# Projecting three tiles of the first head block in float32 from host-transposed copies, and splitting w1 by column blocks

## The chip, the cores and the metric

The kernel runs on one core of a Trainium2 chip. The metric is the time of one execution on the device, in microseconds (us). Engines are named as the profile names them: PE (TensorE matmuls), PEld (its weight loads), DVE (VectorE), ACT (ScalarE), POOL (GpSimd) and SP (SyncE, which here issues the DMAs).

## The reference

The input x is 2048 tokens of 512 features, all float32. What is computed is

```
xn = layernorm(x)
s  = attention(xn) @ wo      # 32 heads of 16; token p looks at p, p-2, ..., p-14 (W = 8, dilation 2)
y  = layernorm(xn)
g  = silu(gelu(y @ w1 + b1) @ w2 + b2)      # 512 -> 1376 -> 512
out = x + s * g
```

with q, k, v = xn @ wqkv, logits scaled by 1/4, positions below 0 masked, and softmax over the 8 positions.

## The kernel before

**Tiles and units.** Tokens are split by parity (the dilation is 2) into two halves of 8 tiles, each of 128 tokens. The 32 heads are split into four head blocks of eight. A unit is one half with one head block; there are eight, u = 0 to 7. `qkv(c, hb, u)` projects a unit's 8 tiles into the buffer U[u % 2] (128 partitions, q, k and v side by side), `attention(c, hb, u)` works on it: products and reductions on DVE, exp on ACT, part of the sums on POOL. The MLP is 44 steps, four chunks of 512 tokens by 11 blocks of F: `mlp1` (12 matmuls, gelu on ACT, high and low part), `mlp2` (12 matmuls into four PSUM tiles). `wo_first` and `wo_last` apply wo.

**Split precision.** A float32 operand is scaled by a power of two and split into a float16 high part and a float16 low part; a product is three float16 matmuls (high by high, low by high, high by low). So a tile's projection is 12 matmuls of 384 columns (line 632). The scale is found on the device: a square with accumulation on ACT (lines 465, 383), a sum over partitions by a small float32 matmul against a tile of fours (lines 391, 396), four short DVE operations (402 to 420). High parts come from ACT (483, 436) or DVE (434), low parts from DVE (485, 437).

**The first layer norm.** `ln0` takes the tiles of the first half in groups (GROUPS): statistics on DVE (525, 526), powers on POOL (512, 519), the normalised tile on DVE (564) or ACT (531, 534). The tile is then transposed on PE by four float32 transposes (571) into PSUM and split into the float16 parts of yT (ACT 581, DVE 582). Two tiles, FP = (2, 3), go first: their transposes are copied to SBUF in float32 (577) and multiplied directly with the unscaled float32 weights (line 639, four matmuls a tile), so that unit 0 can begin before its weights are scaled and split. Evictions to U are on ACT (648). U[1] also holds head block 1's raw weights until they are split. The second half's layer norm (`ln1`) transposes by DMA.

**Order.** Every operation is added to a plan (`Plan.add`) with an engine, an assumed duration, a priority and what it reads and writes. `Plan.issue` then plays the plan through: at each step it takes, over all engines, the operation that can start first, among those nearly as early the one of lowest priority number, and so fixes each engine's order of instructions, which buffer of a ring each gets, and the order of SP's DMAs. On the chip each engine works through its order and waits where an operand is late. PE gets fillers (`WAKE`, line 1042: matmuls of fours into a PSUM tile that nobody reads) where the plan has nothing else for it.

**w1.** The host lays w1 out as 128 partitions by four K tiles of 1376 columns. It is loaded in four pieces, squared in four, and split in four (W1C): since a piece is a range of K, the first MLP step needs parts of all of them.

Of the kernel before, what the change touches and what calls it, by code (L numbers as in the profile page):

```python
# [18 lines left out]
P = 128  # L19
# [5 lines left out]
NI = 8  # L25
# [8 lines left out]
W1C = [0, 2048, 4096, 5120, KT * F]  # L34
LAG = 2
# [3 lines left out]
GROUPS = [(2,), (3,), (0, 1), (4, 5), (6, 7)]  # L39
LOADS = [(2, 1), "q0", "q2", (3, 1), (0, 2), (4, 2), (6, 2)]  # L40

FP = (2, 3)

ACT_Y = (0, 1, 4, 5)

W1DVE = (0, 1, 2, 3)
# [6 lines left out]

DVE_LO = range(0, 44)

# [27 lines left out]
class Plan:  # L83
# [76 lines left out]
    def earliest(self, o):  # L160
        t = max(self.free[o.eng], o.ready)
        if o.port:
            t = max(t, self.portfree)
        if o.eng == "sp" and o.nbytes and len(self.landed) >= QUEUE:
            t = max(t, self.landed[-QUEUE])
        return t

    def place(self, o, t):

        if o.eng == "sp":  # L170
            if not o.nbytes:
                return t
            self.free["sp"] = t + o.issue
            self.dma = max(self.dma, t + o.issue + 0.3)
            self.dma += o.nbytes / (o.rate if self.dma > SLOW else 265e3)
            end = self.dma + o.tail
            self.landed.append(end)
            return end
# [78 lines left out]
MARGIN = {"pe": 0.2, "dve": 0.15, "act": 0.05}  # L257
# [3 lines left out]
QUEUE = 8  # L261

PW2, PS2 = 0.9, 0.74
PWQ1, PW1 = 0.7, 0.75
# [4 lines left out]
WAKE = 4  # L269
WAKE0 = 22  # L270
# [6 lines left out]
PFP = 0.62  # L277
# [13 lines left out]
def tile_mixer(ctx, tc, a_x, a_wqkv, a_wo, b_w1, b_b1, b_w2, out):  # L291
# [21 lines left out]
    def act(n, fn, r, w, aps=1, **k):  # L313
        pl.add("act", 0.07 + n * ACT1 + 0.093 * aps, fn, r, w, **k)
# [13 lines left out]
    fours = sb.tile([P, P], F32, name="fours")  # L328
    nc.vector.memset(fours, 4.0)
    halves = sb.tile([P, 16], F32, name="halves")  # L330
# [8 lines left out]
    w1 = sb.tile([P, 2, KT, F], F16, name="w1")  # L339
# [18 lines left out]
    R_w = Ring(sb, [P, 16], F32, 8, "lw")  # L358
# [27 lines left out]
    def total(dst, dkey, cols, n, ckeys, late=False):  # L386

        b = (R_ps if late else R_z[0]).new()
        if n == 2:
            for k in range(2):  # L390
                pl.add("pe", 0.15, lambda k=k: nc.tensor.matmul(
                    b.t[:, 0:1], fours, cols()[:, k:k + 1], start=(k == 0), stop=(k == 1)),
                    [ckeys[k]], [b], prio=min(pl.prio, PTOT))
            n = 1
        else:
            pl.add("pe", 0.3, lambda: nc.tensor.matmul(b.t[:, 0:n], fours, cols()[:, 0:n], start=True,
                                                       stop=True), ckeys, [b], prio=min(pl.prio, PTOT))
        src, skey = (lambda: b.t[:, 0:1]), b
        if n > 1:
# [3 lines left out]
                                               op0=ALU.max, op1=ALU.min), [skey], [dkey])  # L403

    def half_exp(ss, skey):
# [4 lines left out]
                                                      op=ALU.logical_shift_right), [skey], [b])  # L410
        return h, b

    def up(dst, dkey, h):

        dve(1, lambda: nc.vector.tensor_scalar(dst.bitcast(I32), h[0](), -TWO23, 205.0 * TWO23,
                                               op0=ALU.mult, op1=ALU.add), [h[1]], [dkey])
# [43 lines left out]
    def prep_q(hb):  # L460
# [9 lines left out]
        with pl.fuse():  # L470
            total(lambda: ssq[:, hb:hb + 1], ("ssq", hb), lambda: col.t, 2, [(col, 0), (col, 2)],
                  late=hb > 1)
            h = half_exp(lambda: ssq[:, hb:hb + 1], ("ssq", hb))
            up(qsc[:, hb, 0:1], ("qs", hb), h)
            down(qsc[:, hb, 1:2], ("qi", hb), h, 24.0)
        st = 1 if hb == 0 else 2
# [14 lines left out]
    cpos = [2, 3, 0, 1, 4, 5, 6, 7]  # L491


    def factors(n, mv, mk, cdst, ckeys, bias=True, close=None, pp=None, **k):
# [19 lines left out]
        with pl.fuse():  # L514
            dve(n, lambda: nc.vector.tensor_scalar(a0(), V(), EPS, None, op0=ALU.add), mk, [(A, 0)])
            dve(n, lambda: nc.vector.reciprocal(a1(), a0()), [(A, 0)], [(A, 1)])
            dve(n, lambda: nc.vector.tensor_tensor(a1(), a1(), V(), op=ALU.mult), [(A, 1)] + mk, [(A, 1)])
            dve(n, lambda: nc.vector.tensor_scalar(a1(), a1(), EPS, None, op0=ALU.add), [(A, 1)], [(A, 1)])
# [4 lines left out]
    def stats(mv, a, key, x, xkeys, **k):  # L523
        st = R_bn.new()
        dve(512, lambda: nc.vector.bn_stats(st.t, x()), xkeys, [st], port=False)  # L525
        dve(8, lambda: nc.vector.bn_aggr(mv()[:, a], st.t), [st], [key], port=False, c=0.08, **k)
# [11 lines left out]
    yF = {}  # L538

    def ln0(ii, xs, xkeys):  # L540
        n = len(ii)
        first, way = dict(prio=PLN + pl.prio * 1e-3), dict(prio=PLN + 0.03 + pl.prio * 1e-3)
        mvb = R_w.new()
        mv = lambda: mvb.t.rearrange("p (i s) -> p i s", s=2)
        mk = [(mvb, a) for a in range(n)]

        behind = [("yd", i) for i in (2, 3) if n > 1]
        fz = pl.fuse()
        for a in range(n - 1):
            with pl.fuse():  # L550
                stats(mv, a, mk[a], xs[a], [xkeys[a]] + behind)
        fz.__enter__()
        stats(mv, n - 1, mk[n - 1], xs[n - 1], [xkeys[n - 1]] + behind)
        rb = factors(n, mv, mk, cT[:, 0, cpos[ii[0]]:cpos[ii[0]] + n], [("c", 0, i) for i in ii],
                     ii[0] in ACT_Y, lambda: fz.__exit__(None, None, None), **{"pp": first["prio"]})
        for a, i in enumerate(ii):
            y = R_f.new()
            o = (i % 4) * P
            dst = yT[i // 4]
            if ii[0] in ACT_Y:  # L560
                with prio(PLN + 0.04):
                    y_act(xs[a], rb, a, [xkeys[a]], lambda y=y: y.t, y, ("y_", i))
            else:
                dve(512, lambda a=a, y=y: nc.vector.tensor_scalar(
                    y.t, xs[a](), mv()[:, a, 0:1], rb[0].t[:, a:a + 1], op0=ALU.subtract,
                    op1=ALU.mult), [xkeys[a], (rb[0], 0)] + mk, [y, ("yd", i)], f=0.72, **first)
            b = R_z[1 + i % 3].new()

            def tr(b=b, y=y):
                for k in range(KT):  # L570
                    nc.tensor.transpose(b.t[:, k * P:(k + 1) * P], y.t[:, k * P:(k + 1) * P], ident)
            pe(4, P, tr, [y], [b], fp32=2, **first)
            p3 = lambda b=b: b.t.rearrange("p (k t) -> p k t", k=KT)
            hi, lo = dst[:, 0, :, o:o + P], dst[:, 1, :, o:o + P]
            if i in FP:
                yf = yF[i] = R_L.new()
                act(512, lambda b=b, yf=yf: nc.scalar.copy(yf.t, b.t), [b], [yf], aps=0, **way)
                p3, b, way2 = (lambda yf=yf: yf.t.rearrange("p (k t) -> p k t", k=KT)), yf, dict(prio=PFP)
            else:
                way2 = way  # L580
            act(512, lambda p3=p3, hi=hi: nc.scalar.copy(hi, p3()), [b], [("yh", 0, i)], aps=0, **way2)
            dve(512, lambda p3=p3, hi=hi, lo=lo: nc.vector.tensor_tensor(  # L582
                lo, p3(), hi, op=ALU.subtract), [b, ("yh", 0, i)], [("y", 0, i)], port=i in FP, **way2)

# [24 lines left out]
    IORD, IORD0 = [2, 3, 1, 4, 5, 6, 7, 0], [2, 3, 0, 1, 4, 5, 6, 7]  # L609

    def qkv(c, hb, u):
        ub = u % 2
        U3 = U[ub].rearrange("p (s e) -> p s e", e=P)
        cs = R_cs.new()
        act(NI, lambda: nc.scalar.activation(cs.t, cT[:, c], AF.Identity, scale=qsc[:, hb, 1:2]),
            [("c", c, i) for i in range(NI)] + [("qi", hb)], [cs], prio=PEV) if u else [
            dve(len(g), lambda q=cpos[g[0]], n=len(g), g=g: nc.vector.tensor_scalar(
                cs.t[:, q:q + n], cT[:, c, q:q + n], 1.0 / YS if g[0] in FP else qsc[:, hb, 1:2], None, op0=ALU.mult),
# [617 lines left out]
```

## Time and profile before

| | us |
|---|---|
| median of 3 runs | 420.17 (419.83 to 420.49) |
| the profiled execution | 419.94 |
| its span in the profile | 418.2 |
| PE busy | 408.5 |
| DVE busy | 384.2 |
| ACT busy | 214.8 |
| POOL busy | 111.4 |

The profile is of one execution. A row of the timeline gives the start, the duration from the first to the end of the last of a run of equal instructions, the engine, the line, what is written from what is read, and how many; in brackets the idle time ahead of it and what ended it. A row of the windows gives the stretch and its length, then the busy time and count of PE, PEld, DVE, ACT and POOL, the clock granted to PE, the share of the DMA engines and GB/s. A group row has a line's instructions of one shape: busy time in all, mean ns of one, idle time ahead. The execution's own time is 1.74 us above its span.

### The profile page before, as it was taken

What the parts mean: (1) busy time and instruction counts of PE and PEld (TensorE: products, weight loads), DVE (VectorE), ACT (ScalarE), POOL (GpSimd) and SP (SyncE); (2) the same over time, 40 slices, a digit from 0 to 9 for tenths busy, and PEclk for the clock granted to TensorE, in tenths of its full rate; (3) what the DMA queues carried; (4) which work ended last, traced back from release to release, by engine and by line L of the source; (5) the groups of instructions that cost most, each with busy time, mean ns of one, the idle gap of its engine ahead of it and who ended that gap; (6) DMA issues with size and microseconds to landing.
All of it is one profiled execution on the core that took longest, in us unless ns stands there. A gap on an engine that the chain in (4) does not pass through costs nothing.

```text
span 418.2 us, 5558 instructions
## 1 busy us (share of the span) xinstructions
PE 408.5 (98%) x2095; PEld 208.7 (50%) x2095; DVE 384.2 (92%) x403; ACT 214.8 (51%) x321; POOL 111.4 (27%) x126
## 2 busy tenths in 40 slices
PE   7799999999999999999999999999999999999995
PEld 4466544444554455445544654465455544444442
DVE  5958999999999999899998999999999998999953
ACT  6799972762539764843396335134212573263500
POOL 5310200004341525042504250433124304520031
PEclk9999999999999999999999999999999999999999
DMA  8963260030036247621271025104505343016132
GB/s 292 415 225 106 77 213 2 16 137 0 0 97 175 72 100 171 135 59 27 71 206 63 2 87 125 52 26 130 184 0 152 117 130 119 2 34 217 27 125 100
DMA packets 42650, 44.83 MB, mean 107 GB/s; under 512 B 27480, under 2 KB 27920, under 8 KB 42112
## 3 DMA queue, kind: packets, MB, share of 16 engines
q1 hardware_dynamic: 42624, 44.49, 35.1%
q8 instruction: 16, 0.26, 0.3%
q14 instruction: 10, 0.08, 0.1%
HBM read 23.53 MB, written 7.34 MB: 74 GB/s over the span
## 4 chain that ended last, share of the span: by engine, by line
PE 81%; DVE 11%; ACT 4%; issue 1%; DMA 1%; SPq 0%; POOL 0%; DVEq 0%
PE ps L632 24%; PE z L943 24%; PE ps L898 22%; PE ps L815 7%; PE z L815 2%; DVE w L437 2%; DVE prod L691 2%; DVE L L694 2%; ACT w L436 1%; DMA prod<-in_A_x_dram 1%; DVE bn L525 1%; PE pl L632 1%; DVE h L921 1%; PE pl L815 1%; DVE w L434 1%
## 5 line engine op out<-in xcount | busy, mean ns | idle before, releaser
L898 PE MATMUL ps<-yT,w 128*128 128x512 f16 (+1 forms) x528 | 120.8, 379 | 0.0
L632 PE MATMUL ps<-wq,yT 128*128 128x384 f16 x708 | 117.9, 326 | 1.0 <-DVE yT L582 1.0
L943 PE MATMUL z<-w,h 128*128 128x512 f16 x480 | 110.8, 379 | 0.0
L632 PEld LDWEIGHTS <-yT 128*128 128x128 f16 x744 | 72.8, 98 | 49.0 <-DVE yT L582 1.3
L898 PEld LDWEIGHTS <-w 128*128 128x128 f16 (+1 forms) x528 | 52.9, 100 | 61.3 <-issue 0.5
L915 ACT ACTIVATE ps<-ps,b1T,hsc 128x512 f32<-128x512 f32 (+1 forms) x44 | 32.8, 748 | 87.1 <-PE ps L898 86.9
L691 DVE TENSOR_TENSOR prod<-U 128x2048 f32<-128x2048 f32 x32 | 73.0, 2285 | 2.8 <-DMA U<-U 1.7
L943 PEld LDWEIGHTS <-h 128*128 128x128 f16 x480 | 47.0, 98 | 55.4
L694 DVE TENSOR_REDUCE L<-prod 128x128 f32<-128x2048 f32 x32 | 72.9, 2280 | 0.4
L648 ACT ACTIVATE U<-ps,cs 128x384 f32<-128x384 f32 x61 | 35.1, 578 | 65.1 <-PE ps L632 63.6
L749 DVE TENSOR_TENSOR prod<-pl,U 128x2048 f32<-128x2048 f32 x28 | 63.2, 2281 | 4.3 <-POOL prod L759 4.2
L759 POOL TENSOR_TENSOR prod<-prod,prod 128x2048 f32<-128x2048 f32 x7 | 31.7, 4528 | 100.0 <-DVE prod L749 100.0
L769 POOL TENSOR_TENSOR prod<-prod 128x1024 f32<-128x1024 f32 x14 | 32.9, 2347 | 0.0
L768 POOL COPY gate<-prod 1x1 f32<-1x1 f32 x21 | 5.5, 263 | 92.7 <-DVE prod L691 89.9
L815 PE MATMUL ps<-wo,oT 128*128 128x512 f16 x132 | 29.6, 379 | 0.0
L921 DVE SCALAR_TENSOR_TENSOR h<-ps,hsc,h 128x512 f16<-128x512 f32 x40 | 29.5, 741 | 0.1
L815 PEld LDWEIGHTS <-oT 128*128 128x128 f16 x189 | 18.5, 98 | 22.1
L918 ACT ACTIVATE h<-ps,hsc 128x512 f16<-128x512 f32 x40 | 27.2, 683 | 0.8
L744 DVE TENSOR_TENSOR prod<-prod,prod 128x2048 f32<-128x2048 f32 x9 | 20.5, 2278 | 0.0
L915 ACT ACT_TABLE_LOAD x11 | 14.1, 1283 | 6.1 <-PE ps L898 5.9
L769 POOL TENSOR_TENSOR prod<-prod,prod 128x1024 f32<-128x1024 f32 x7 | 16.4, 2348 | 0.0
L732 ACT ACTIVATE o<-prod,osc 128x1024 f16<-128x1024 f32 (+1 forms) x9 | 9.5, 1052 | 11.8 <-POOL prod L769 7.4
(155 smaller groups left out, 346.8 us busy)
## 6 DMA issues: line engine op xcount, KB each, us to landing
f<-in_A_x_dram SPq DMA_DIRECT2D x31, 256.0 KB, 3.2
U<-U SPq DMA_DIRECT2D x16, 392.0 KB, 3.8
gd<-f SPq DMA_DIRECT2D x12, 256.0 KB, 2.2
oT<-in_B_w_dram SPq DMA_DIRECT2D x2, 1024.0 KB, 11.9
yT<-in_B_w_dram SPq DMA_DIRECT2D x2, 1024.0 KB, 12.6
f<-gd SPq DMA_DIRECT2D x8, 256.0 KB, 3.2
out_dram<-f SPq DMA_DIRECT2D x8, 256.0 KB, 2.6
out_dram<-U SPq DMA_DIRECT2D x7, 256.0 KB, 2.0
```

Source lines behind the costliest of these rows:

```text
L632: nc.tensor.matmul(b.t[:, 0:384], y[:, s, k, o:o + P], wq[:, hb, t, k], start=(n == 0), stop=(n == 11))
L648: act(384, lambda i=i, b=b: nc.scalar.activation(U3[:, i:i + 31:15, :], b.t[:, 0:384].rearrange("p (t e) -> p t e", t=3), AF.Identity, sca ...
L691: dve(2048, lambda p2=p2, g=g: nc.vector.tensor_tensor(p2(), q, slots(Ut, KH, 2 * g), op=ALU.mult), qk + [("kh", ub, 0), ("kh", ub, 1), (" ...
L694: dve(2048, lambda pr=pr, g=g: nc.vector.tensor_reduce(L3()[:, 2 * g:2 * g + 2], pr.t.rearrange("p (r f d) -> p r f d", r=2, d=DH), AX.X, ...
L749: dve(2048, lambda: nc.vector.tensor_tensor(pr.t.rearrange("p (r f d) -> p r f d", r=2, d=DH), A3()[:, 2 * g:2 * g + 2].rearrange("p r (f ...
L759: pool(4.75, lambda: nc.gpsimd.tensor_tensor(acc.t, acc.t, p1.t, op=ALU.add), [acc, p1], [acc])
L769: nc.gpsimd.tensor_tensor(x.t[:, 0:1024], x.t[:, 0:1024], y(), op=ALU.add)
L815: nc.tensor.matmul(b.t, oT[:, hb, i // 4, s, i % 4], wo[:, t, hb], start=(hb == 0 and n == 0), stop=(hb == last and n == 2))
L898: nc.tensor.matmul(b.t[0:M], w1[:, s, k, f * P:f * P + M], yT[ch][:, t, k], start=(n == 0), stop=(n == 11))
L915: act(512, lambda: nc.scalar.activation(b.t[0:M], b.t[0:M], AF.Gelu_apprx_tanh, bias=b1T[0:M, f:f + 1], scale=hsc[0:M, 1:2]), [b, ("b1T",) ...
L921: dve(512, lambda: nc.vector.scalar_tensor_tensor(lo()[0:M], b.t[0:M], hsc[0:M, 2:3], hi()[0:M], op0=ALU.mult, op1=ALU.subtract), [b, hk], ...
L943: nc.tensor.matmul(z.t, hl[s][0:K, t * P:(t + 1) * P], w2[0:K, w, f], start=(f == 0 and n == 0), stop=(f == NF - 1 and n == 2))
```

## The change

- The tiles that are multiplied in float32 are now three, FP = (5, 6, 7). The host also passes a transposed copy of these three tiles, `A_xt`. They are loaded into U[1]. `center` takes each token's mean off on the device: a sum over the four K tiles on DVE (or, for tile 7, two additions on POOL), a float32 matmul with a tile of 1/512 on PE, a subtraction on DVE. `direct` multiplies the centred copy with head block 0's raw weights, four float32 matmuls a tile; the factor of the layer norm goes into the eviction's scale. These three tiles are still loaded untransposed too, normalised, transposed on PE and split, later, since head block 1 and the MLP need them.
- Tiles 0 to 4 are transposed on PE as before, from the normalised tile in place in its load buffer; tiles 0, 2, 3, 4 are normalised on ACT, the others on DVE. `ln0` is parted: the first factor for four groups, the second (`second`) for two batches.
- SP's order is changed: three transposed copies, both blocks' weights and the x tiles one by one, then w1, w2.
- Head block 1's weights are scaled and split earlier, and its projection follows in the order 0 to 7 right after block 0's.
- w1 is laid out by column blocks of 128, each with its four K tiles beside each other, and split in seven pieces (W1P) of one or two blocks; the first two high parts are on DVE, the other five on ACT, and the last five have a priority just below the MLP's own operations.
- Sums over partitions read the upper 16 bits of the float32 column as bfloat16, and fours is bfloat16.
- The plan's assumed durations are changed, and its limit on the DMA queue counts bytes in flight instead of eight DMAs.

```diff
-FP = (2, 3)
-ACT_Y = (0, 1, 4, 5)
-W1DVE = (0, 1, 2, 3)
+W1P = [(0, 1), (1, 2), (2, 4), (4, 6), (6, 8), (8, 10), (10, 11)]
+W1FIRST = 2
+FP = (5, 6, 7)
+GROUPS = [(0,), (1,), (2, 3, 4), (5, 6, 7)]
+BATCHES = [(0, 1, 2, 3, 4), (5, 6, 7)]
+LOADS = [("t", 5), ("t", 6), ("q", 0), ("q", 2), ("x", 0), ("x", 1), ("t", 7), ("q", 4), ("q", 6), ("x", 2), ("x", 3),
+         ("x", 4), ("x", 5), ("x", 6), ("x", 7)]
+Y_ENG = {0: "act", 1: "dve", 2: "act", 3: "act", 4: "act", 5: "dve", 6: "dve", 7: "dve"}
+W1ENG = ["dve", "dve", "act", "act", "act", "act", "act"]
...
+    def center(i):
+        n = FP.index(i)
+        b = R_ps.new()
+        x3 = xt[i]
+        f = R_f.new()
+        f3 = lambda: f.t[:, 0:2 * P].rearrange("p (k t) -> p k t", k=2)
+        if n < 2:
+            dve(512, lambda: nc.vector.tensor_reduce(f3()[:, 0], x3.rearrange("p k t -> p t k"), AX.X, ALU.add),
+                [("xt", i)], [f], port=False, c=0.45)
+        else:
+            pool(0.75, lambda: nc.gpsimd.tensor_tensor(f3(), x3[:, 0:2], x3[:, 2:4], op=ALU.add), [("xt", i)], [f])
+            pool(0.45, lambda: nc.gpsimd.tensor_tensor(f3()[:, 0], f3()[:, 0], f3()[:, 1], op=ALU.add), [f], [f])
+        pe(1, P, lambda: nc.tensor.matmul(b.t[:, 0:P], mean1, f3()[:, 0], start=True, stop=True), [f], [b], fp32=6, prio=0.04)
+        m = lambda: b.t[:, 0:P].rearrange("p (o t) -> p o t", o=1).to_broadcast([P, KT, P])
+        dve(512, lambda: nc.vector.tensor_tensor(x3, x3, m(), op=ALU.subtract), [b, ("xt", i)], [("xc", i)], port=False, c=0.16)
...
+    def direct(i):
+        b = pb[i] = ([R_pl] + R_z[1:])[FP.index(i)].new()
+        for k in range(KT):
+            pe(1, 384, lambda k=k: nc.tensor.matmul(
+                b.t[:, 0:384], xt[i][:, k], stq[0]()[:, k * 384:(k + 1) * 384], start=(k == 0), stop=(k == KT - 1)),
+                [("xc" if i in XC else "xt", i), ("stq", 0, k)], [b], fp32=4.5, holds=stkey[0], after=pl.users([b]))
...
-                nc.tensor.matmul(b.t[0:M], w1[:, s, k, f * P:f * P + M], yT[ch][:, t, k],
+                nc.tensor.matmul(b.t[0:M], w1[:, s, f * 512 + k * M:f * 512 + (k + 1) * M], yT[ch][:, t, k],
...
-    for n in range(4):
-        c0, c1 = W1C[n:n + 2]
-        split(w1f[0][:, c0:c1], w1f[1][:, c0:c1], s1[n], hsc[:, 0:1],
-              [s1k[n], ("hsc0",)] + [("oTst", 2 * n)] * (n < 2), ("w1", n), "dve" if n in W1DVE else "act", n=c1 - c0)
+    for m, (f0, f1) in enumerate(W1P):
+        n = min(f0 // 4, 2) if f0 < 10 else 3
+        c0, c1 = 512 * f0, min(512 * f1, KT * F)
+        with prio(PW1 if m < W1FIRST else PR_H + 1 + (10 * f0 - 25) * 1e-6):
+            split(w1f[0][:, c0:c1], w1f[1][:, c0:c1], lambda n=n, c0=c0, c1=c1: s1[n]()[:, c0 - W1C[n]:c1 - W1C[n]], hsc[:, 0:1],
+                  s1k[n] + [("hsc0",)] + [("w1h", j) for j in range(4) if W1C[j] < c1 and W1C[j + 1] > c0], ("w1", m),
+                  W1ENG[m], n=c1 - c0)
...
+    lay["A_xt"] = inputs["A_x"].reshape(P, NI, DIL, KT, P)[:, list(FP), 0].transpose(1, 3, 2, 0)
+    w1 = inputs["B_w1"].reshape(KT, P, F)
+    lay["B_w1"] = _np.concatenate([w1[:, :, f * P:(f + 1) * P].transpose(1, 0, 2).reshape(P, -1) for f in range(NF)], 1)
```

More of the change, by code (lines that the diff above doesn't have):

```diff
@@ L163, in earliest @@
             t = max(t, self.portfree)
[L164 to L165 removed]
+        if o.eng == "sp" and o.nbytes:
+            left = FLIGHT
+            for end, n in reversed(self.landed):
+                left -= n
+                if left < 0:
+                    t = max(t, end)
+                    break
         return t
```

299 lines of the change are left out of this document (162 added, 137 removed).

## The prediction

> **What bounds the kernel now.** I read the page first, then PE's timeline, then the stretches (busy time by window).
>
> ```profile
> span 418.2 us, 5558 instructions
> PE 408.5 (98%) x2095; PEld 208.7 (50%) x2095; DVE 384.2 (92%) x403; ACT 214.8 (51%) x321; POOL 111.4 (27%) x126
> PE 81%; DVE 11%; ACT 4%; issue 1%; DMA 1%; SPq 0%; POOL 0%; DVEq 0%
> ```
>
> PE is busy for 98% and carries 81% of the chain that ended last. A busy PE need not do needed work, though: the fillers (L1042) count too. So I look at where PE starts to be fed without a break.
>
> ```profile
> 1.05 4.23 PE L1042 MATMUL z<-fours 128*128 128x256 bf16 x19 [1.05 <-DVE s L1097]
> 11.31 2.85 PE L639 MATMUL ps<-prod,L 128*128 128x384 f32 x8
> 13.99 0.38 PE L1042 MATMUL z<-fours 128*128 128x256 bf16 x2
> 18.96 1.48 PE L632 MATMUL ps<-wq,yT 128*128 128x384 f16 x8 [1.02 <-DVE yT L582]
> 20.70 1.09 PE L571 MATMUL z<-ident,f 128*128 128x128 f32 x8 [0.27 <-DVE yT L582]
> 48.74 7.93 PE L898 MATMUL ps<-yT,w 128*128 128x512 f16 x36
> 65.15 2.75 PE L898 MATMUL ps<-yT,w 128*128 128x512 f16 x12
> 88.59 0.28 PE L391 MATMUL ps<-s,fours 128*128 128x1 f32 x2
> 89.45 2.75 PE L943 MATMUL z<-w,h 128*128 128x512 f16 x12
> 403.21 9.88 PE L815 MATMUL z<-wo,oT 128*128 128x512 f16 x45
> 412.92 0.82 PE L865 MATMUL z<-wo,oT 128*128 128x256 f16 x6
> ```
>
> PE's rows follow each other without idle time from 20.70 to the end of the last one at 413.74, but for a few tenths between 88.59 and 89.45. The end is therefore the start of that run, plus PE's work, plus a tail of 4.5 us; whatever saves time must fill the first 20.7 us better or take work off PE. DVE is the second bound:
>
> ```profile
> 0.00:35.00 35.00, 30.12 (x170) 18.96 (x171) 22.90 (x76) 28.18 (x51) 10.88 (x22) 1.00 0.75 284
> 35.00:57.10 22.10, 22.10 (x127) 12.32 (x126) 21.75 (x39) 19.67 (x34) 2.51 (x1) 1.00 0.42 127
> 57.10:397.40 340.30, 339.96 (x1725) 169.90 (x1723) 330.21 (x275) 166.93 (x238) 92.91 (x99) 1.00 0.31 87
> 65.02 2.27 DVE L694 TENSOR_REDUCE L<-prod 128x128 f32<-128x2048 f32 x1
> 396.70 0.75 DVE L734 SCALAR_TENSOR_TENSOR o<-prod,osc,o 128x512 f16<-128x512 f32 x1 [0.79 <-ACT o L732]
> oT<-o SPq DMA_TRANSPOSE x9, 4.4
> ```
>
> DVE's number (the fourth in a row, after PE and PEld) is 330.21 of 340.30 us from the first attention product to the last low part, at 397.45. That part's transpose, 4.4 us in the list of DMA issues, must land before the z-group's tenth matmul, about 405.2. So there are some 3 us, the most that PE could gain if DVE gained nothing.
>
> **When the operands land.** SP's order is now: transposed tiles 5 and 6, two halves of head block 0's weights, x tiles 0 and 1, transposed tile 7, half of block 1's weights, x2, x3, the other half, x4 to x7, then w1. So 786 kB of copies go into the queue, ahead of w1 and mostly ahead of the x tiles.
>
> ```profile
> 0.00:2.00 2.00, 0.95 (x5) 0.71 (x6) 0.18 (x2) 1.27 (x1) 1.40 (x9) 1.00 0.07 23
> 2.00:5.00 3.00, 3.00 (x16) 1.99 (x14) 1.48 (x7) 0.43 (x2) 2.32 (x5) 1.00 0.99 346
> 5.00:7.00 2.00, 1.40 (x10) 0.99 (x8) 1.16 (x4) 1.96 (x5) 0.77 (x2) 1.00 0.96 287
> 7.00:9.00 2.00, 1.87 (x6) 1.06 (x6) 1.76 (x12) 1.49 (x4) 0.60 (x2) 1.00 1.04 379
> 9.00:12.00 3.00, 2.35 (x11) 1.27 (x10) 2.90 (x7) 2.60 (x6) 0.96 (x1) 1.00 1.07 435
> 3.35 0.69 DVE L525 BATCH_NORM_STATS2 bn<-prod 128x6 f32<-128x512 f32 x1 [2.35 <-DMA prod<-in_A_x_dram]
> 6.63 0.69 DVE L525 BATCH_NORM_STATS2 bn<-prod 128x6 f32<-128x512 f32 x1 [0.66 <-DMA prod<-in_A_x_dram]
> ```
>
> The last column is GB/s. Summed, 1.08 MB are in by 5 us, 1.66 by 7, 2.42 by 9, 3.72 by 12. The first load (0.26 MB) is used at 3.35, when 0.51 MB had moved; the fourth (1.31 MB in all) at 6.63, at 1.55. So a load can be used once its own cumulated bytes plus 0.24 MB have moved: tile 5 at 3.35, tile 6 4.1, the weight halves 5.25 and 6.6, x0 7.4, x1 8.1, tile 7 8.8, x2 10.3, x3 10.9, x4 12.5.
> The Trainium skill, "DMA: Bandwidth & Descriptors", Specifications, gives an HBM limit of about 358 GB/s a core; the row from 9 to 12 us has 435, so here the trace is above it. By the page x3 would come 0.4 us later, and the sum would lose some 0.25 us.
>
> **The part up to the MLP, step by step.** Step lengths are start-to-start:
>
> ```profile
> 11.44 0.66 DVE L525 BATCH_NORM_STATS2 bn<-prod 128x6 f32<-128x512 f32 x1
> 12.23 0.66 DVE L525 BATCH_NORM_STATS2 bn<-prod 128x6 f32<-128x512 f32 x1
> 22.87 1.88 DVE L582 TENSOR_TENSOR yT<-z,yT 128x512 f16<-128x512 f32 x3
> 15.71 1.67 DVE L485 SCALAR_TENSOR_TENSOR wq<-prod,qsc,wq 128x384 f16<-128x384 f32 x3
> 8.20 2.13 ACT L483 ACTIVATE wq<-prod,qsc 128x384 f16<-128x384 f32 x4 [0.47 <-DVE qsc L415]
> 14.19 0.29 ACT L531 ACTIVATE lw<-lw,lw 128x1 f32<-128x1 f32 x1 [1.78 <-DVE lw L526]
> 15.24 0.28 ACT L531 ACTIVATE lw<-lw,lw 128x1 f32<-128x1 f32 x1
> 21.65 1.06 ACT L581 CAST yT<-z 128x512 f16<-128x512 f32 x2
> 19.76 1.90 ACT L383 ACTIVATE w<-oT 128x2048 bf16<-128x2048 f32 x1
> 38.55 1.04 ACT L648 ACTIVATE U<-ps,cs 128x384 f32<-128x384 f32 x2
> 43.96 2.17 ACT L436 ACTIVATE w<-yT,zsc 128x1024 f16<-128x1024 f32 x2
> 13.46 0.70 POOL L512 TENSOR_TENSOR lw<-lw,halves 128x2 f32<-128x2 f32 x1 [3.50 <-DVE lw L508]
> L714 DVE TENSOR_REDUCE mx<-L 128x64 f32<-128x512 f32 x8 | 5.5, 682 | 0.5
> ```
>
> That gives: statistics 0.8, low part 0.63, weights' low part 0.53, ACT's high parts 0.51, a normalised tile on ACT 1.05, a 2048 square 1.89, an eviction 0.47, a 1024 cast 1.04. On PE, with 0.15 taken off each row for the last one's latency, a tile's fp32 product takes 2.7 (8 records of 0.34), a tile's four transposes 0.55, a 384-column matmul 0.1625, one of 512 columns 0.216, a sum over partitions 0.14.
>
> New operations have no row. The centring's sums over 512 elements I take at the 0.68 of L714 (ends: 0.3 and 2.3, those of reductions a quarter and four times as long), the subtraction at 0.63 like L582. The mean's fp32 matmul over 128 columns lies between a transpose, 0.14, and a product, 0.68; a third of the product's columns gives 0.25. A bf16 sum lies between 0 and 0.14; I take 0.06.
>
> PE runs 15 fillers (0.223 each) to 4.4; two means and two subtractions let tile 5's product start at 5.85 (before: 7.13). Products 5 and 6 run to 11.6, hiding the mean of 7. DVE has x0's statistics at 7.4, the four short scale operations by 9.0, x1 by 10.3, x2, then x3 at 11.15, the subtraction of tile 7 at 11.95, y1 to 13.1, one weight part, x4 to 14.45, low part 0, the rb input at 15.1; POOL's power of three columns (0.70 for two; I take 0.86) ends at 16.15. PE: transposes of 0 at 12.15, product 7 from 12.7 to 15.95 around transposes of 1, tile 0 to 17.35. ACT makes y2, y3, y4 from 16.2 to 19.3, so PE has transposes 2 and 3, half of tile 1 and then nothing from 19.65 until 20.65: tiles 2 and 4 share a PSUM bank, and DVE's low part of 2 comes late. It reaches 23.15 and waits again: tile 3 needs the bank of product 5, whose eviction stands on ACT behind y2 to y4, two casts, the first w1 square, another cast, a scale and a 768 cast: 16.2 + 3.15 + 1.0 + 1.9 + 0.5 + 0.2 + 0.9 + 0.5 = 24.4. From 24.45 on it has work without a break: 36 matmuls of block 0 that are left and 96 of block 1, 132 x 0.1625 = 21.45, three tiles of transposes 1.65, a filler and sums 0.4. So the first MLP group starts at 47.95. Before: 48.74. **Gain 0.8.** PE's work up to there grew by 0.9 (third fp32 tile 2.7 - 1.95, three means 0.75, sums -0.6), its idle and filler time fell by 1.7.
>
> **From there to 65 us.** Before, 48.74 to 65.15 is six groups of 12 (15.54) and 0.87 of fp32 sums. After: 15.54, 0.24 of bf16 sums, a filler 0.2, and two waits, since most of w1's high parts moved from DVE to ACT (four casts of 1.04 and one of 0.45) and the gelu stands among them. The fourth group needs the bank that DVE frees at 56.2 (0.3); the fifth one freed behind a 2.2 us reduce, at 64.65 (0.55). It starts at 64.7 instead of 65.15. **Gain 0.45.** DVE ends its fourth attention operation and fourth low part of h at 65.3; before, the row at 65.02 is that fourth operation and ends at 67.2. It is 1.9 us ahead, so it does not bind. The w1 layout lets the first group go with one piece, ready at 38; its other pieces stay ahead of PE by several us.
> Edits costed at nothing: SP's halo copies of block 0 wait for ACT's last eviction, at 33.2, with b1 and the last w2 tiles queued behind them; those are used from 42 on, 5 us later than they land. Block 1's evictions wait until the copies in its buffer are read, which product 7 has done by 15.95, 20 us earlier. POOL's two adds for tile 7 have from 8.8 to 10.0; a microsecond more is covered by x3's statistics, which stand before the subtraction until 11.95.
>
> **Later.**
>
> The sums from 88.59 to the group at 89.45 take 0.86 us, of which two pairs of records at 0.14 with their latency are some 0.5 and the rest a wait for ACT that stays. Two bf16 sums in their place: **gain 0.4.** Beyond that the order of PE's groups is nearly the same, and I count no wait of PE there, as the rows of before have none. Sum: 0.45 + 0.4 = 0.86, say 0.9. The profiled execution took 419.94 (span 418.2 and 1.74 around it), so 419.1 for its like; the median of the runs is 0.23 above it, so 419.3.
>
> **The rivals.**
> *The waits vanish.* If ACT runs the w1 square earlier or DVE's low part comes in time, the waits at 19.65, 23.15, 56 and 64 go: 1.0 + 1.3 + 0.85, about 3.2, so 416.1. For it: these waits hang on single short operations. Against: both engines stand full from 16 to 28 us in my walk.
> *ACT becomes the bound (slower).* Place: 42 to 62 us, where 4.6 us of casts join the queue ahead of the gelu and the evictions. Before, ACT had 2.4 us free between 35 and 57.1 (19.67 of 22.10). What does not fit, 2.2 us, up to all 4.6, lands on PE through banks freed late: 421.5 to 423.9. It is slower than before from 0.9 us of delay on beyond the 0.85 counted, and measurably from 1.7.
> *The loads come late (slower).* If the 287 GB/s of 5 to 7 us lasts, x3 lands near 13 instead of 10.9 and everything behind it moves 2.1 us: 421.4. Against: the rows rise to 435.
> *The clock.* Fillers step by 0.223 us at the start, two at 13.99 by about 0.11: half rate first, although the clock column says 1.00. If a wait brought half rate back for as long as the start's 3.4 us or so, it would cost 1.7: 421.0. Against: right after 1.02 us of idle time the eight matmuls at 18.96 took 1.48, full rate. The Trainium skill, "TensorE: Matmul & The Clock Gate", Part 1, has it that an idle window of about 3.4 us halves the clock; by that my waits are too short.
> *It does not do what it says:* in the order of PE's instructions block 1 follows block 0 as before, rather than sharing tiles with it; I have counted nothing for it.
>
> **The numbers.** About 0.2% (0.84 us) is what a measurement here can tell from no change. My walk 0.48, with its own range 417.8 to 420.8 (landings and new operations, 1.5 either way): 0.27 of it faster, 0.19 same, 0.02 slower. Waits vanish 0.26, faster. ACT 0.15, slower. Loads 0.08: 0.03 same, 0.05 slower. Clock 0.03, slower. Together faster 0.53, same 0.22, slower 0.25. The range runs from 415.8 (all waits gone, and the three means at a transpose's price, 0.1 less each) to 422.7 (the middle of ACT's case).
>
> **What would show it.** Right: the first fp32 product near 5.9; PE idle near 20 and 23; first MLP group near 48; gapless from 65. Wrong: ACT's gelu more than 2 us behind PE's group, statistics waiting for DMA after 11 us, or gaps of PE after 65 us, where I counted none.

## The result, and the profile after

| | before | changed |
|---|---|---|
| median of 20 runs each | 420.44 us | 419.57 us |
| lowest and highest | 419.68 to 421.29 | 419.02 to 420.59 |
| ratio, with its 95% interval | | 0.9983 (0.9976 to 0.999) |
| profiled execution, span | 419.94, 418.2 | 420.04, 418.3 |

The changed kernel is 0.17% faster by the ratio; its median is 0.87 us (0.21%) lower. The two profiled executions say otherwise, by 0.1 us; why, a second profile of the same kernel shows (e13 below). First the page of the changed kernel: span, busy time of the engines, and the chain's shares.

```profile
span 418.3 us, 5534 instructions
...
PE 408.4 (98%) x2082; PEld 207.4 (50%) x2082; DVE 386.3 (92%) x395; ACT 213.6 (51%) x322; POOL 110.7 (26%) x124
...
PE 68%; DVE 15%; issue 7%; ACT 5%; DMA 3%; SPq 1%; POOL 0%; DVEq 0%; ACTq 0%
```

PE is as busy as before, but its share of the chain fell from 81% to 68%, DVE's rose from 11% to 15%: the chain now leaves PE somewhere. PE's timeline of the changed kernel tells where (start, duration, what, and in brackets the wait; `...` stands for rows left out, and an L956 row with fewer than 12 products, here and below, is part of a group: the stretch asked for ends there, or a sum stands between):

```profile
6.93 0.88 PE L578 MATMUL pl<-prod,U 128*128 128x384 f32 x2 [0.59 <-DMA prod<-in_A_wqkv_dram]
...
19.47 0.66 PE L641 MATMUL z<-ident,prod 128*128 128x128 f32 x4 [0.38 <-ACT prod L622]
...
20.97 0.82 PE L698 MATMUL ps<-wq,yT 128*128 128x384 f16 x4 [0.85 <-ACT yT L644]
...
24.65 0.27 PE L1102 MATMUL z<-fours 128*128 128x256 bf16 x1 [0.35 <-DVE yT L645]
...
25.32 1.46 PE L698 MATMUL pl<-wq,yT 128*128 128x384 f16 x8 [0.41 <-ACT U L708]
...
48.26 7.93 PE L956 MATMUL ps<-yT,w 128*128 128x512 f16 x36
...
56.37 2.75 PE L956 MATMUL ps<-yT,w 128*128 128x512 f16 x12
...
64.79 1.46 PE L956 MATMUL ps<-yT,w 128*128 128x512 f16 x6 [0.46 <-DVE h L978]
...
85.56 2.75 PE L956 MATMUL ps<-yT,w 128*128 128x512 f16 x12
...
88.15 0.19 PE L403 MATMUL ps<-s,fours 128*128 128x1 bf16 x2
88.20 2.75 PE L992 MATMUL z<-w,h 128*128 128x512 f16 x12
...
203.62 0.81 PE L992 MATMUL z<-w,h 128*128 128x512 f16 x3
...
205.03 2.12 PE L698 MATMUL ps<-wq,yT 128*128 128x384 f16 x12 [0.60 <-DMA yT<-f]
...
216.07 2.75 PE L956 MATMUL ps<-yT,w 128*128 128x512 f16 x12
...
219.06 0.81 PE L992 MATMUL z<-w,h 128*128 128x512 f16 x3 [0.24 <-ACT f L1008]
...
412.85 0.82 PE L926 MATMUL z<-wo,oT 128*128 128x256 f16 x6
```

Read against the rows of before: the first MLP group starts 0.48 us earlier (48.74), the fifth 0.36 (65.15), the group behind the sums 1.25 (89.45). Up to 203.62 nothing is lost. Then two gaps come that before does not have. Three matmuls from 203.62 take 0.65 start to start, so the next could start at 204.27 and starts at 205.03: 0.76. Twelve from 216.07 take 2.59, so 218.66, and the next starts at 219.06: 0.40. Together 1.16, and at the last products the lead is 0.07. The gain of the start was there and was given back in the middle. What PE waits for there are a tile of the second half's layer norm, whose low part DVE finishes at 201.88 and whose transpose lands at 204.99, and ACT's silu that frees a PSUM bank of the MLP, done at 219.01:

```profile
201.02 0.86 DVE L664 TENSOR_TENSOR f<-f,f 128x512 f16<-128x512 f32 x1
...
218.32 0.69 ACT L1008 ACTIVATE f<-z,zsc 128x512 f32<-128x512 f32 x1
```

What the loads did: rows of ACT's and DVE's timeline in the changed kernel (DVE's two centring sums, ACT's square, which is the first use of the weights' first half, and DVE's statistics of tiles 0 and 2), then two stretches, with GB/s last.

```profile
3.35 1.97 DVE L564 TENSOR_REDUCE f<-U 128x128 f32<-128x512 f32 x2 [2.07 <-DMA U<-in_A_xt_dram]
...
6.82 0.84 ACT L477 ACTIVATE wq<-prod 128x768 bf16<-128x768 f32 x1 [4.81 <-DMA prod<-in_A_wqkv_dram]
...
8.47 0.70 DVE L542 BATCH_NORM_STATS2 bn<-prod 128x6 f32<-128x512 f32 x1 [1.51 <-DMA prod<-in_A_x_dram]
...
11.52 0.69 DVE L542 BATCH_NORM_STATS2 bn<-prod 128x6 f32<-128x512 f32 x1 [0.41 <-DMA prod<-in_A_x_dram]
```

```profile
2.00:5.00 3.00, 3.00 (x15) 2.04 (x13) 1.65 (x2) 0.01 (x1) 2.05 (x3) 1.00 0.86 274
...
9.00:12.00 3.00, 3.00 (x12) 1.73 (x10) 2.39 (x13) 1.92 (x4) 2.00 (x4) 1.00 1.04 395
```

The weights' first half was usable at 6.82 instead of 5.25, tile 0 at 8.47 instead of 7.4, tile 2 at 11.52 instead of 10.3: from 2 to 5 us 274 GB/s were moved, not 346.

### The profile page after: what moved, and what is told of

Its sections match the earlier page's. It is cut to its first block, busy times and chain, and to the rows that moved or that the text cites. A ratio compares the mean times of both kernels' runs of the same rounds, so it can differ in the third digit from the quotient of the medians.

```text
span 418.3 us, 5534 instructions
## 1 busy us (share of the span) xinstructions
PE 408.4 (98%) x2082; PEld 207.4 (50%) x2082; DVE 386.3 (92%) x395; ACT 213.6 (51%) x322; POOL 110.7 (26%) x124
## 4 chain that ended last, share of the span: by engine, by line
PE 68%; DVE 15%; issue 7%; ACT 5%; DMA 3%; SPq 1%; POOL 0%; DVEq 0%; ACTq 0%
PE z L992 19%; PE ps L698 19%; PE ps L956 18%; PE ps L876 7%; DVE prod L810 3%; PE z L876 2%; DVE prod L752 2%; DVE w L449 2%; DVE h L978 2%; DMA prod<-in_A_x_dram 2%; PE pl L698 1%; DVE f L664 1%; DVE L L755 1%; DMA U<-U 1%; DVE prod L805 1%
## 5 line engine op out<-in xcount | busy, mean ns | idle before, releaser
L956 PE MATMUL ps<-yT,w 128*128 128x512 f16 (+1 forms) x528 | 120.8, 379 | 0.5 <-DVE h L978 0.5
L698 PE MATMUL ps<-wq,yT 128*128 128x384 f16 x696 | 115.9, 326 | 1.4 <-ACT yT L644 0.8
L698 PEld LDWEIGHTS <-yT 128*128 128x128 f16 x732 | 71.1, 98 | 50.6 <-issue 1.2
L956 PEld LDWEIGHTS <-w 128*128 128x128 f16 (+1 forms) x528 | 52.9, 100 | 61.5 <-issue 0.8
L752 DVE TENSOR_TENSOR prod<-U 128x2048 f32<-128x2048 f32 x32 | 74.3, 2326 | 2.1 <-DMA U<-U 1.0
L708 ACT ACTIVATE U<-ps,cs 128x384 f32<-128x384 f32 x58 | 33.6, 581 | 58.1 <-PE ps L698 57.9
L829 POOL COPY gate<-prod 1x1 f32<-1x1 f32 x21 | 4.4, 211 | 88.4 <-DVE prod L752 88.4
```

Of the source, the lines that this page charges most:

```text
L698: nc.tensor.matmul(b.t[:, 0:384], y[:, s, k, o:o + P], wq[:, hb, t, k], start=(n == 0), stop=(n == 11))
L708: act(384, lambda i=i, b=b: nc.scalar.activation(U3[:, i:i + 31:15, :], b.t[:, 0:384].rearrange("p (t e) -> p t e", t=3), AF.Identity, sca ...
L752: dve(2048, lambda p2=p2, g=g: nc.vector.tensor_tensor(p2(), q, slots(Ut, KH, 2 * g), op=ALU.mult), qk + [("kh", ub, 0), ("kh", ub, 1), (" ...
L956: nc.tensor.matmul(b.t[0:M], w1[:, s, f * 512 + k * M:f * 512 + (k + 1) * M], yT[ch][:, t, k], start=(n == 0), stop=(n == 11))
```

## The experiments

All were run against the kernel before (medians 420.23 to 420.48). Letters of theories are those of the expectation that stands above each result.

**e1: the changed kernel with float32 sums; e2: the kernel before with bfloat16 sums.** Orders unchanged.

```diff
 e1
-    b.t[:, 0:1], fours[:, 0:P], top()[:, k:k + 1], ...
+    b.t[:, 0:1], fours32, cols()[:, k:k + 1], ...
 e2
-    b.t[:, 0:1], fours, cols()[:, k:k + 1], ...
+    b.t[:, 0:1], fours16, top()[:, k:k + 1], ...
```

> The changed kernel with its sums over partitions in float32 again, every engine's order as in the changed kernel. Theory S (the bf16 sums carry the gain): 13 sums cost PE 0.14 us each instead of 0.03 and the two near 88 us get back their wait, so the first MLP group starts near 48.8 instead of 48.26, the fifth group near 65.4, and the time is 1.0 to 1.7 us above the changed kernel, level with or above the kernel before (ratio 0.999 to 1.003). Rival F (the front carries it): the group starts near 48.4 and the time is at most 0.5 us above the changed kernel (0.9983 to 0.9995).

> The kernel before with the bf16 sums alone, every engine's order as before. Theory S: the first MLP group starts near 48.2, the sums at 61.7, 62.9 and 88.6 shrink from 1.6 us to 0.3 to 0.6, and the time falls by 1.0 to 1.7 us (ratio 0.996 to 0.9976), as much as the whole change or more. Rival F: at most 0.5 us (0.9988 to 1).

e1: 420.16 us, ratio 0.9994 (0.9982 to 1.0005), 0.59 above the changed kernel's median: between what S (1.0 to 1.7) and F (at most 0.5) expected, and the intervals of the two ratios overlap. In its profile the first float32 product starts 0.28 later (7.21), unit 2's projection 0.97 later (104.71 against 103.74) and the last products 0.73 later (413.58), so the float32 sums cost some 0.7 in front of the gaps and some 0.45 at the end. e2: 420.26, ratio 0.9996 (0.9987 to 1.0006): no gain that can be told from noise, as F expected. Its profile began late: the first product starts 0.61 later than before's (7.74 against 7.13), the last products 0.49 later. So 0.12 is left of what the sums save, and PE's row shows what took the rest:

```profile
65.85 2.32 PE L901 MATMUL ps<-yT,w 128*128 128x512 f16 x10 [0.82 <-DVE h L924]
```

The kernel before has no wait at that group. There DVE's low part of h comes just in time (it ends at 65.10, the group starts at 65.15), so PE can't use what cheaper sums give it; in the changed kernel DVE is ahead from 65 us on, and they count.

**e3: the second half's layer norm a whole unit earlier.**

```diff
-    pl.prio = PR_U * 2 + 900
+    pl.prio = PR_U + 950
     ln1()
```

> The changed kernel with the second half's layer norm at priority 1950 instead of 2900, so that its transposes come earlier; the orders are those of the changed kernel up to about 70 us. Theory G (what the front and the sums save, 1.25 us by 104 us, is lost again in two waits at 204 and 219 us, the first for the transposes): both waits go and the time falls 0.8 to 1.2 us below the changed kernel (ratio 0.9955 to 0.9965). Rival D (DVE is the bound there, the wait only moves): the wait stands elsewhere and the time is within 0.4 us of the changed kernel.

422.0, ratio 1.004 (1.0028 to 1.0052): slower, which neither G nor D expected. The gaps at 204 and 219 us are gone, but DVE loses more, in its waits (total, times, longest) and then in PE's row at the end:

```profile
DVE prod L810 <- POOL prod L820: 5.6, 4, 1.9
DVE h L978 <- ACT h L976: 4.1, 6, 1.0
```

```profile
398.63 2.10 PE L876 MATMUL pl<-wo,oT 128*128 128x512 f16 x9 [0.77 <-DVE prod L848]
```

In the changed kernel DVE waited 1.8 for that POOL addition and 2.6 for h. The last unit's attention ends later, the planner puts 27 products of wo_last's z tiles ahead of the last ones of the first tiles, and DVE's last operation ends 1.7 us later than in the changed kernel (416.92 against 415.25). PE's last products start at 412.87, as in the changed kernel: the loss lies behind them, in DVE's evictions, as in e5 below.

**e5: w1's high parts on DVE. e6: the same, and another order in wo_last.**

```diff
 e5, e6
-W1ENG = ["dve", "dve", "act", "act", "act", "act", "act"]
+W1ENG = ["dve"] * 7
 e6: tiles 5 to 7 of wo_last are added to the plan behind tile 2, and read what its last products write
-               [("wo", k) for k in (0, 2)] + [("A", 7)] * (rings[i] is R_pl), [b], ...
+               [("wo", k) for k in (0, 2)] + [("A", 7)] * (rings[i] is R_pl) + (tiles[2:3] if i > 4 else []), [b], ...
```

> The changed kernel with all seven high parts of w1 on DVE instead of the last five on ACT. Theory A (the casts delay the gelu, and with it the fourth and fifth MLP groups, by 0.8 us): the waits of PE at 56 and 64.5 us shrink to below 0.3, the fifth group starts before 64.4, DVE's attention operations come 2 to 3 us later; the time falls by up to 0.5 us or, if DVE then binds, rises by 1 to 2 us. Rival (neither is near the bound): within 0.3 us.

> The kernel with w1's high parts on DVE, and in wo_last the first nine products of tiles 5, 6 and 7 are placed behind the last three of tile 2. In the run with w1's high parts on DVE alone, PE had no wait after 45 us and ended 2.0 us earlier than in the changed kernel (411.5 against 413.7), but the span was only 0.3 us shorter: the plan put 27 products of the z tiles ahead of the last products of the first three tiles, DVE stood idle for 4.4 us to 405.06 and then worked without a pause to the end. Theory C (the order at the end alone kept that gain): DVE's first eviction of wo_last begins near 401.0 to 401.5, PE still ends near 411.5, and the span is 416.1 to 416.6, the median 417.9 to 418.4. Rival (the end is bounded by DVE's attention of the last unit and by the stores, whatever the order): 419.5 to 419.9 as with the high parts on DVE alone.

e5: 419.76, ratio 0.9992 (0.9981 to 1.0004), no gain over the changed kernel. e6: 418.87, ratio 0.9956 (0.994 to 0.9971), span 416.1. DVE's first eviction of wo_last and PE's last products, in e5 and then in e6:

```profile
405.06 2.07 DVE L939 SCALAR_TENSOR_TENSOR U<-ps,osc,U 128x512 f32<-128x512 f32 x3 [4.42 <-PE ps L876]
...
410.69 0.82 PE L926 MATMUL z<-wo,oT 128*128 128x256 f16 x6
```

```profile
401.21 2.07 DVE L945 SCALAR_TENSOR_TENSOR U<-ps,osc,U 128x512 f32<-128x512 f32 x3 [0.58 <-PE ps L876]
...
410.72 0.82 PE L932 MATMUL z<-wo,oT 128*128 128x256 f16 x6
```

PE ends at the same time in both, 2.1 us ahead of the changed kernel, with no wait after 45 us. In e5 DVE stood idle for 4.42 us because PE did other products first, and the end slid behind DVE's evictions; in e6 it did not, and the span is 1.9 us shorter. The span is as expected, the median 0.5 above what was expected from it.

**e4: half the weights ahead of tile 6. e9: the square of w1 behind the evictions.** Each is one edit to the changed kernel, at the start.

```diff
 e4
-LOADS = [("t", 5), ("t", 6), ("q", 0), ("q", 2), ...
+LOADS = [("t", 5), ("q", 0), ("t", 6), ("q", 2), ...
 e9
-    sumsq(lambda n=n: cw1.t[:, n:n + 1], (cw1, n), s1[n], s1k[n],
+    sumsq(lambda n=n: cw1.t[:, n:n + 1], (cw1, n), s1[n], s1k[n] + [("v", 0, i) for i in FP],
```

> The changed kernel with one edit in SP's order: the first half of head block 0's weights is loaded ahead of the transposed tile 6 instead of behind it. In the changed kernel the first float32 product began at 6.93 us because that half was usable at 6.82. Both theories expect the first product near 5.9 to 6.2 and tile 6's centring about 1 us later. Theory A (what PE gains at the start is taken back by later waits that the planned order and DVE set, at 64.8, 204 and 219 us): the first MLP group begins 0 to 0.6 us earlier than 48.26, but the end moves by less than 0.3 us, 419.3 to 419.9. Theory B (PE bounds the kernel from start to end, so that a gain at the start is a gain at the end): the end moves with the first MLP group, 418.8 to 419.2.

> The changed kernel with one edit: ACT's square of w1 may only begin when the evictions of the three float32 products are done. In the changed kernel PE waited 0.35 us at 24.65 and 0.41 at 25.32, which the prediction put down to an eviction of a float32 product queued behind that square. If that is so, these two waits, 0.76 us together, go. Theory A (gains of the start are taken back later): the first MLP group begins up to 0.7 us earlier, the end moves by less than 0.3 us, 419.3 to 419.9. Theory B (PE bounds from start to end): 418.8 to 419.1. If the waits stay, the square was not their cause.

e4: 417.59, ratio 0.9927 (0.9915 to 0.9939). e9: 418.2, ratio 0.9943 (0.9931 to 0.9955). PE's rows of e4, then of e9:

```profile
6.14 1.89 PE L578 MATMUL pl<-prod,U 128*128 128x384 f32 x4
...
46.93 7.93 PE L956 MATMUL ps<-yT,w 128*128 128x512 f16 x36
...
55.69 2.53 PE L956 MATMUL ps<-yT,w 128*128 128x512 f16 x11 [0.72 <-DVE h L978]
...
84.27 2.75 PE L956 MATMUL ps<-yT,w 128*128 128x512 f16 x12
...
410.39 0.82 PE L926 MATMUL z<-wo,oT 128*128 128x256 f16 x6
```

```profile
6.38 1.04 PE L578 MATMUL pl<-prod,U 128*128 128x384 f32 x2
...
47.08 0.81 PE L956 MATMUL ps<-yT,w 128*128 128x512 f16 x3
...
56.32 1.89 PE L956 MATMUL ps<-yT,w 128*128 128x512 f16 x8 [1.28 <-DVE h L978]
...
84.90 2.75 PE L956 MATMUL ps<-yT,w 128*128 128x512 f16 x12
...
411.02 0.82 PE L926 MATMUL z<-wo,oT 128*128 128x256 f16 x6
```

The group that starts at 85.56 in the changed kernel starts 1.29 earlier in e4 and 0.66 in e9. The last products come 2.46 and 1.83 earlier, so another 1.17 in both: neither has the gaps at 204 and 219. So a lead of PE at 85 us is kept to the end (theory B; A falls), and the two gaps belong to the changed kernel's plan, which an edit elsewhere may shuffle (e4 and e9 lose them, e7 keeps them). That the gaps would go was not foreseen: both medians lie below the range of either theory. In e9 the waits at 24.65 and 25.32 are gone: the square was their cause. In e4 they have shrunk to one of 0.20, at 24.09. Of e9's 1.18 at the first MLP group, 0.55 is the first product, which came earlier in this execution with its weights; 0.52 is lost again up to 85 us, where PE waits for h at 56.32.

**e7: all of w1 split before the MLP begins.**

```diff
-W1FIRST = 2
+W1FIRST = 7
```

> The changed kernel with all seven pieces of w1 split at the priority of the first two, so ahead of the MLP's own operations, as in the kernel before; the column layout stays. Theory D (the column blocks are worth something, because ACT and DVE can split the later blocks behind the first MLP steps): the first MLP group begins 0.5 to 2 us later than 48.26 or its third and fourth group wait as much, and the median is 420.2 to 421.5. Rival (the split was hidden behind unit 1's projection anyway, as in the kernel before, where the first MLP group began at 48.74 with no wait): the first group within 0.3 us of 48.26 and the median 419.2 to 419.9.

419.77, ratio 0.9987 (0.9975 to 0.9998); the first MLP group at 48.37, its fourth with a wait of 0.40. The rival is right: the changed kernel's later priority for five of the seven pieces is worth nothing that these runs show. The layout by column blocks itself stayed in e7 and was not undone.

**e10: the second half's layer norm slightly earlier.** The order of PE stays up to about 130 us, and at the end.

```diff
-    pl.prio = PR_U * 2 + 900
+    pl.prio = PR_U * 2 + 650
     ln1()
```

> The changed kernel with one number altered: the second half's layer norm gets the priority of unit 1 plus 650 instead of plus 900. Everything that PE does up to about 130 us keeps its order, and so does wo_last; only the middle is planned anew. In the changed kernel PE had lost 1.16 us in two gaps, 0.76 at 204 us (transposes of that layer norm) and 0.40 at 219 us, and was 1.25 us ahead of the kernel before until then. Four other plans whose edits lie at the start had neither gap. Theory E (the two gaps belong to this one plan of the middle and are all that the change loses): without them the first MLP group still begins at 47.6 to 48.4 by the load's chance, and the median is 418.2 to 418.7, span of the profile 417.0 to 417.4 if the load is as late as in the changed kernel. Rival (the second half's layer norm and the attention share DVE, and a wait comes elsewhere in the middle or at the end, as when it was put a whole unit earlier): 419.3 to 422.

419.02, ratio 0.9962 (0.9949 to 0.9975), span 416.4. PE's rows:

```profile
6.25 0.88 PE L578 MATMUL pl<-prod,U 128*128 128x384 f32 x2 [0.28 <-DMA prod<-in_A_wqkv_dram]
...
64.11 2.10 PE L956 MATMUL ps<-yT,w 128*128 128x512 f16 x9 [0.46 <-DVE h L978]
...
410.99 0.82 PE L926 MATMUL z<-wo,oT 128*128 128x256 f16 x6
```

In this execution the first product came 0.68 before that of the changed kernel's profile, and so did the group at 64.11; the end is 1.86 earlier, 0.68 and 1.18 for the gaps that are gone. The profile bears theory E out to 0.02 us. The median moved by only 0.55, and lies above the expected 418.2 to 418.7; the profiled execution (418.18) was the fastest of the six. Of that difference I have no row.

**e11: e4 and e9 together. e12: e11, and e6's two edits.**

> The changed kernel with both edits at the start together: the first half of the weights ahead of the transposed tile 6, and ACT's square of w1 behind the evictions of the three float32 products. Theory B (PE bounds the kernel from start to end): the first MLP group begins near 46.5, against 46.93 with the loads alone and 47.08 with the square alone. What is gained there over these two counts only so far as the wait for h's low part at 55 to 57 us, 0.72 and 1.28 us in these two runs, doesn't grow by as much; it is expected to. So the median is 417.2 to 417.7, about that of the loads alone (417.59). Rival (the start is PE's alone, gains add): 416.5 to 417.1.

> The changed kernel with four edits: the two at the start (weights ahead of tile 6, the square behind the evictions), w1's high parts on DVE, and the order of wo_last. With w1's high parts on DVE PE had no wait between 45 us and the end. Theory B with the wait for h's low part removed by relieving ACT: the first MLP group near 46.5, no wait at 55 to 57 us, the end 1.2 to 1.6 us ahead of the kernel with the high parts on DVE and the order of the end (416.1 span), so a span of 414.6 to 415.2 and a median of 416.4 to 417.0. Rival (the wait at 55 to 57 us is DVE's work on h and w1 and grows with more high parts on DVE): 417.3 to 418.0.

e11: 417.99, ratio 0.9937 (0.9926 to 0.9949), where 417.2 to 417.7 was expected. e12: 418.86, ratio 0.9959 (0.9946 to 0.9972), span 416.8 where 414.6 to 415.2 was expected. The gains of the start do not add. In e11 the first MLP group starts at 47.42, later than with either edit alone: the wait that the square's edit removes is already down to 0.20 in e4, and in this execution tile 0 was usable 0.24 later than in e4 (8.18 against 7.94), which is half of the difference. Then PE waits 0.73 us for h at 71.95. In e12 the first MLP group starts at 46.74, the earliest of all, and it is taken back at one place:

```profile
74.32 2.28 DVE L755 TENSOR_REDUCE L<-prod 128x128 f32<-128x2048 f32 x1
...
76.51 0.74 DVE L984 SCALAR_TENSOR_TENSOR h<-ps,hsc,h 128x512 f16<-128x512 f32 x1
...
77.31 2.75 PE L962 MATMUL ps<-yT,w 128*128 128x512 f16 x12 [1.81 <-DVE h L984]
```

DVE's low part of h, 0.74 us long, stands behind an attention reduction of 2.28, and PE waits for the bank that it frees. In e11 it is the same: h's low part at 71.16 stands behind a reduction of 2.28 at 68.96. So theory A has its place too: e11 leads the changed kernel by 1.60 us at the fifth MLP group (63.19) and by 0.66 at 85 us, e12 by 2.45 (62.34) and 0.49; no version here leads by more than e4's 1.29 there. e4 has the lowest median, 0.73% below the kernel before by the ratio; its interval (0.9915 to 0.9939) overlaps those of e9 and e11.

**e13: the changed kernel again, unedited.**

> The changed kernel once more, unedited. In the profiles of runs with its order of loads the first float32 product began between 6.23 and 7.21 us, and the changed kernel's own profile (6.93, 420.04 us) was slower than its median (419.57). Theory F (that product's start, the load's chance, is what makes one execution of this kernel differ from another, and PE carries it to the end): if the product begins at 6.93 - d here, the first MLP group begins at 48.26 - d, and the profiled execution takes 420.04 - d as far as the gaps at 204 and 219 us stay 1.16 us together; the median is again 419.3 to 419.8. Rival (DVE or the transposes take up an early start, so that the gaps grow by what the start gains): 420.0 whatever d.

419.39, ratio 0.9983 (0.9968 to 0.9998). ACT's first use of the weights and PE's rows of this profile:

```profile
5.84 0.84 ACT L477 ACTIVATE wq<-prod 128x768 bf16<-128x768 f32 x1 [3.83 <-DMA prod<-in_A_wqkv_dram]
...
6.44 0.94 PE L578 MATMUL pl<-prod,U 128*128 128x384 f32 x2
...
47.90 2.32 PE L956 MATMUL ps<-yT,w 128*128 128x512 f16 x10
...
64.42 1.89 PE L956 MATMUL ps<-yT,w 128*128 128x512 f16 x8 [0.46 <-DVE h L978]
...
204.57 2.12 PE L698 MATMUL ps<-wq,yT 128*128 128x384 f16 x12 [0.51 <-DMA yT<-f]
...
412.38 0.82 PE L926 MATMUL z<-wo,oT 128*128 128x256 f16 x6
```

The first product is 0.49 earlier than in the first profile, the first MLP group 0.36, the fifth 0.37, the last products 0.47, and the execution took 419.56 instead of 420.04, 0.48 less. Both gaps are there again, 0.67 and 0.41, worked out as above. So theory F for these two: they differ by when the first product starts, and PE carries that to the end. The loads are only part of it: here the first weights were usable 0.98 earlier (5.84 against 6.82), but the product came only 0.49 earlier, because tile 5's subtraction ends at 6.10, and the mean of tile 6 (from 5.80) and a filler (6.23) stand ahead of it on PE. In the nine profiles with this order of loads the first product started between 6.23 and 7.21; in seven of them 0.11 or 0.12 behind ACT's first square of those weights, in e6 and e13 0.5 to 0.6 behind it.

## Why the prediction was right, and which steps failed

It said 419.3 with a gain of 0.86 on the profiled time; the medians give 419.57 and 0.87. That the numbers are so close is partly chance: PE gained more than was counted, two gaps that were not counted took most of that back, and the baseline lay higher. In e13, whose profiled execution is typical of the changed kernel, the lead over before's profile is 0.84 at the first MLP group (predicted 0.8), 0.73 at the fifth (0.45), and 1.62 behind the sums (0.86), when the projection of unit 2 begins at 103.37 instead of 104.99; the gaps take 1.08 of it, and 0.54 is left at the last products. The rest of the 0.87 is that before's profiled execution was 0.5 us below the median of 20 runs, not 0.23 as against the first three. Which edits of the start brought its part of the gain (the third float32 tile, the copies, the order of loads, the evictions), no run separates; in e7 the later priority of w1's pieces was worth nothing that shows.

- **PE bounds from 20.7 us on: right behind 85 us.** e4, e9, e10 and e13 carry the lead that PE has there to the end within 0.1 us, once the gaps are counted. Between the first MLP group and 85 us it holds for e4, e10 and e13, but e9 lost 0.52 and e12 more, to DVE's low parts of h.
- **The landings: too early.** Usable "once its own cumulated bytes plus 0.24 MB have moved" holds only at the rate of before. The weights' first half was usable at 6.82, in e13 at 5.84, against 5.25; the first product started at 6.93 and 6.44 against 5.85. The Trainium skill ("DMA: Bandwidth & Descriptors", Specifications) gives an HBM limit of about 358 GB/s a core; as in the trace of before, the changed kernel is above it, at 395 from 9 to 12 us. The lateness arose earlier, from 2 to 5 us, at 274.
- **The centring: too cheap.** Its two sums took 1.97 together, so 0.98 each, not 0.68; subtraction 0.69 for 0.63. That cost nothing in the first profile, where the weights were later still. In e13 they were there at 5.84, and the product waited for the centring until 6.44; in e11 it waits 0.23 us for the subtraction and starts at 6.09.
- **The waits up to the MLP: right in place and cause, off in size.** 0.38 and 0.85 at 19 to 21 us (predicted 1.0), 0.35 and 0.41 at 24 to 25 (predicted 1.3); e9 confirms that the square caused the latter. First MLP group predicted at 47.95, found at 48.26 and 47.90.
- **From there to 65 us: right.** A fourth group at 56.37 (56.2) and a wait of 0.46 (0.55); the fifth group at 64.79 and 64.42 (64.7). DVE's fourth low part of h ends at 65.39 (65.3).
- **The sums near 88 us: mis-sized, 0.81 instead of 0.4.** "A wait for ACT that stays" did not stay: ACT's square of wo was done at 87.2 instead of 89.2.
- **"No wait of PE there": the step that failed.** The prediction compared the order of PE's groups, which hardly changes, and not when the operands of the second half come. Of that half's layer norm, the last low part but one ends on DVE at 201.88 in the changed kernel, at 179.42 before; its transpose lands at 204.99, and PE wants it at 204.27. (The last one ends at 204.69, before at 189.07.) The second gap is ACT's: its silu stands behind three table loads of 1.28 us each between 213.02 and 218.32. e10, where that layer norm comes earlier, has neither gap. DVE's lead of 1.9 us at 65 us was spent by then, and the last attention part ended at 401.03 instead of 397.45; PE shows no wait for it.
- **The rivals.** ACT was busy for 14.80 of 15 us between 50 and 65, but PE was idle for only 0.53 of them. The loads came late, but by 1.2 us at tile 2, not 2.1. The waits did not vanish; e9 shows that two of them could. No half rate behind the waits: four matmuls behind 0.85 us of idle time took 0.82.

## What to carry to other kernels

In this kernel, with one engine 98% busy, what it gains at the start it has at the end, until the next engine's queue holds it up; look there for a short operation (an eviction that frees a bank) behind a long one. A planner's order is part of every edit: two gaps of 1.16 us came and went with edits 180 us away, so follow one PE instruction through both traces, at several places, before a cause is named. Where the first loads differ between executions by as much as the change brings, compare two profiles by the start of the first product, not by their spans.

## What the runs showed of the hardware

- The same order of loads gave 234 to 305 GB/s from 2 to 5 us in nine profiles, and moved the first product by 1.0 us.
- A float32 reduction of 512 elements on DVE over an index with a stride of 128 elements (L564, sums, 128 results) took 0.98 us, one over the innermost index (L775, maxima, 64 results) 0.68. Which of these differences makes it, no run separates.
- A DVE operation with two SBUF operands, 0.68 us elsewhere, was stretched to 2.47 while POOL added; it ended 0.54 us behind POOL's end:

```profile
182.13 0.68 DVE L664 TENSOR_TENSOR f<-f,f 128x512 f16<-128x512 f32 x1
...
185.19 4.53 POOL L820 TENSOR_TENSOR prod<-prod,prod 128x2048 f32<-128x2048 f32 x1 [17.62 <-DVE prod L810]
...
187.79 2.47 DVE L664 TENSOR_TENSOR f<-f,f 128x512 f16<-128x512 f32 x1
```

  The Trainium skill, "SBUF — State Buffer", SBUF: two separate sides, says that DVE and GpSimd share a port pair under an exclusive lock for the whole instruction, the loser blocking; the row agrees, 187.79 + 2.47 = 190.26 against 185.19 + 4.53 = 189.72.
- A bfloat16 matmul of one column takes 0.03 us of PE, start to start (88.15 to 88.20 for two). A float32 one, two records in the trace, takes 0.14 in the kernel before when it stands alone (62.92 to 63.06), and some 0.23 behind another (61.83 to 62.06).
- An ACT_TABLE_LOAD on ACT took 1.28 us; three of them stand between 213.02 and 218.32 in the changed kernel.
